# Decode attention, four layers: K tiles of two layers in halves, second query weights in two transfers, uneven first K pieces, mean from PSUM

## The chip, the cores and the metric

The kernel runs on one core of a Trainium2 chip. The metric is the device time of one launch in microseconds. A profile of one execution comes with the kernel; its engines are PE (TensorE matmuls), DVE (VectorE), ACT (ScalarE), POOL (GpSimd) and SP (SyncE, which here only issues DMAs and waits for their conditions).

## The reference

Four attention layers decode one token: A, B, A, B. A and B have their own K and V caches and weights; layer 2 uses A's again and layer 3 B's. All is bf16, with D = 640, 32 heads, 8192 keys and a head width of 192.

```python
def _A_ref(x, k_cache, v_cache, wq, wo):        # _B_ref computes the same
    q = (x @ wq).reshape(B, Sq, Hq, Dh).transpose(0, 2, 1, 3)
    scores = jnp.einsum("bhqd,bhkd->bhqk", q, k) * (Dh ** -0.5)
    p = _softmax(scores, axis=-1)
    o = jnp.einsum("bhqk,bhkd->bhqd", p, v)
    return o.transpose(0, 2, 1, 3).reshape(B, Sq, Hq * Dh) @ wo
x = x + _A_ref(_layernorm(x), A_k_cache, A_v_cache, A_wq, A_wo)
x = x + _B_ref(_layernorm(x), B_k_cache, B_v_cache, B_wq, B_wo)
x = x + _A_ref(_layernorm(x), A_k_cache, A_v_cache, A_wq, A_wo)
x = x + _B_ref(_layernorm(x), B_k_cache, B_v_cache, B_wq, B_wo)
```

K and V of one layer are 201 MB, so nearly all of the work is to stream them through the core once.

## The kernel before

**Tiles and slots.** A layer goes over 16 pairs of heads. A pair's K is a tile of 128 partitions (64 for each head) with 128 keys of 192 numbers on each, 6144 KB, and so is its V. SBUF holds eight slots of 3072 KB, half a tile each. A tile loads as one DMA where its two slots are adjacent and the tile is listed as joint, and otherwise as two. Slots 5 to 7 hold A's query weights (two and a half slots) from layer 0 to layer 2, and the second half of slot 7 the first quarter of A's first K tile. So layers 0 and 1 have slots 0 to 4, and their tiles are given slots by the strings `RINGS`, one word for each load, in the order of the plan. The last two V tiles of layer 1 stay in slots 0 to 3 until layer 3 needs them; layer 2 lives with slots 4 to 7, and layer 3 has all eight.

**The order.** `plan` is the order of the loads, and SP issues them strictly in that order; before each it waits for the steps in `before[n]`, which free what the slot held. A joint tile waits for both its slots. `steps` is the order of the work, which each compute engine follows in its own queue.

**The work of a pair.** *m* (`products`, L672, for each half): DVE multiplies the K half in place by the broadcast query (L687, in two or four chunks), and PE sums it over the 192 columns into a PSUM bank by matmuls with the identity (L702 and the helper's L72); the half is then free. *s* (`softmax`): DVE reduces the sums to scores (L742), takes the maximum, and ACT exponentiates (L757). *v* (`values`): PE multiplies the probabilities by V (L799 and L72); both halves are then free. *e* (`gather`): DVE picks and sums the diagonal blocks (L823, L825), and the row goes into `rows`. After every fifth pair, *wc* (`columns`) turns five pairs' outputs into columns and *wo* multiplies them by 2400 KB of output weights; the last pair's part is *wol* (480 KB). In layer 1 the last of the three is split: the first ten rows (*wo*), then five (*wob*).

**Between layers.** After *wol*, DVE adds the result to x (L907), sums x and its squares (L495, L496), PE adds over the partitions by a matmul with ones (L498), DVE scales by 1/640 (L501) and subtracts the mean (xb, L511). PE then computes q of the first pair (*lead*, L552), and the q of all other pairs in five rows c = 0 to 4 of the weights (*wq*, three groups of two, two and one rows, L575). Layer 1's query weights are one transfer of 7680 KB into slots 2, 3 and 4 (L440).

**Layer 2's first K tile** comes in quarters. The first is in SBUF already; the second and third go into slot 4, which holds layer 1's last output weights (ten rows, then *wob*, then *wol*, in this order), and the fourth into slot 5, over the first row of A's query weights (L421). The second waits for the ten rows' use, the third for *wol*'s, the fourth for the first group (two rows) of *wq*.

`busy` puts filler matmuls on PE (L487).

Of the kernel before, what the change touches and what calls it, by code (L numbers as in the profile page):

```python
# [69 lines left out]
def matmul_held(t, out, lhsT, rhs, start, stop, size=128, column=0):  # L70
# [10 lines left out]
RINGS = ["01 23 40 12 34 01 23 04 12 34 0 12 34 01 23 40 12 34 01 23 04 1 23 04 12 34 01 23 40 12 34 01 23 4 0 1",  # L81
         "234 01 23 40 12 34 01 23 04 12 34 0 12 34 01 23 40 12 34 01 23 04 1 23 04 12 34 01 23 40 12 34 01 23 4 01"]


def build(nc, A_x, A_k, A_v, A_wq, A_wo, B_x, B_k, B_v, B_wq, B_wo, out):
    _, H, SK, DH = A_k.shape
    D = A_x.shape[-1]
    P = 128
# [26 lines left out]
    with ExitStack() as ctx:  # L115
# [15 lines left out]
        QUARTER = [K0Q, slot[A_WQ - 1][:, 0:TS // 2], slot[A_WQ - 1][:, TS // 2:], slot[A_WQ][:, 0:TS // 2]]  # L131
        rows = sb("rows", [P, QR], BF16)
# [7 lines left out]
        small = sb("small", [P, 82], F32)  # L140
# [9 lines left out]
        neghalf = col(1)  # L150
        s_sb = [sb(f"s_sb{i}", [P, J], F32) for i in range(2)]
# [62 lines left out]
        PO.op(lambda g: g.memset(half33, 0.0))  # L214
        ev_const = PO.op(lambda g: g.memset(neghalf[:], -0.5))
# [35 lines left out]
        for l in range(NL):  # L251
            if l < 2:
                plan.append(("wq", l, 0))
                steps += [("wq", l, g) for g in range(3)]
            elif l == 2:
                steps += [("lead", l, 0, 0), ("wq", l, 0), ("lead", l, 0, 1), ("wq", l, 1), ("wq", l, 2)]
            else:
                both(("wq", l, 0))
            for p in range(NPAIR):
                if l == 0 and p == 0:  # L260
                    plan.append(("kh", l, p))
                if l == 2 and p == 0:
                    plan += [("kq", l, p, i) for i in range(1, 4)]
                else:
                    plan += [("k", l, p, u) for u in range(2)]
                if l == 2 and p == 0:
                    steps.append(("mq", l, p, 0))
                    for i in range(1, 4):
                        steps += [("mq", l, p, i), ("rd", l, p, i - 1)]
                    steps.append(("rd", l, p, 3))  # L270
                else:
                    steps.append(("m", l, p, 0))
                    if l == 2 and p == 1:
                        steps.append(("e", l, 0))
                    steps.append(("m", l, p, 1))
                if p == NPAIR - 1:
                    steps.append(("v", l, p - 1))
                steps.append(("s", l, p))
                if l == 3 and p == 0:
                    both(("wq", l, 1), ("wq", l, 2))  # L280
                if p < NPAIR - 2:
                    if first_load("v", l, p) == (l, p):
                        plan += [("v", l, p, u) for u in range(2)]
                    steps.append(("v", l, p))
                    if l != 2 or p > 0:
                        steps.append(("e", l, p))
                    if p + 1 in (PAIRS_W, 2 * PAIRS_W):
                        b = (p + 1) // PAIRS_W - 1
                        steps.append(("wc", l, b))
                        both(("wo", l, b))  # L290
            for i in (p - 1, p):
                if first_load("v", l, i) == (l, i):
                    plan += [("v", l, i, u) for u in range(2)]
            plan.insert(-2, ("wo", l, 2))
            steps += [("busy", l, 16), ("e", l, p - 1)] if NB[l] else [("e", l, p - 1)]
            steps += [("v", l, p, 0), ("wc", l, 2)] if NB[l] else [("wc", l, 2), ("v", l, p, 0)]
            steps += [("wo", l, 2), ("v", l, p, 1)]
            if NB[l]:
                plan.append(("vq", l))
                steps.append(("e", l, p))  # L300
                both(("wob", l))
            else:
                steps.append(("e", l, p))
            both(("wol", l))
            if l == 3:
                both(("woe", l))
        at = {n: i for i, n in enumerate(steps)}

        def released(n):
# [6 lines left out]
            return at[("wol", n[1]) if n[0] == "wo" and n[2] == 2 and NB[n[1]] else n]  # L316

        place, before, holder = {}, {}, [None] * NSLOT
        for g in range(3):
            place["wq", 0, g], before["wq", 0, g] = A_WQ + g, []  # L320
            holder[A_WQ + g] = ("wq", 2, g)
# [9 lines left out]
        def allot(n):  # L331
# [20 lines left out]
        for n in plan:  # L352
            if n[0] == "wol":
                before[n] = [] if NB[n[1]] else [("wc", n[1], 2)]
            elif n[0] in ("wob", "vq", "woe", "kh"):
                before[n] = []
            elif n[0] == "kq":
                before[n] = [None, ("woa", 1, 2), ("wo", 1, 2), ("wq", 2, 0)][n[3]:n[3] + 1]
                if n[3] == 3:
# [4 lines left out]
                    before["k", 2, 1, 1] = [("kq", 2, 0, 3)]  # L364
# [26 lines left out]
        def last_rows(l):  # L391

            return slot[place[("wo", l, 2)]][:, NW * D:(NW + OI) * D] if NB[l] else rows[:]
# [4 lines left out]
        def transfer(n):  # L398
# [10 lines left out]
            if n[0] == "wob":  # L409
                r0 = o["wo"][2] * PD  # L410
                return SP.op(lambda s: s.dma_start(
                    slot[place[("wo", l, 2)]][:, (NW - NB[l]) * D:NW * D],
# [4 lines left out]
            if n[0] in ("kh", "kq"):  # L417
                h = 2 * pair(l, 0)
                q = n[3] if n[0] == "kq" else 0
                r = w["k"][0, h:h + 2].rearrange("h (p j) d -> (h p) (j d)", j=J)[:, q * TS // 2:(q + 1) * TS // 2]  # L420
                return SP.op(lambda s: s.dma_start(QUARTER[q], r), *free, sem=[semVQ, *semR, semS[A_WQ]][q], inc=16)  # L421
            i = place[n]
            t = slot[i]
            if n[0] in "kv":
# [7 lines left out]
                if whole(*n[:3]):  # L432
                    if n[3] == 1:
                        return landed[n[:3] + (0,)]
                    x = TS // 2 if n[:3] == ("k", 0, 0) else 0
                    f = lambda s: s.dma_start(pool[:, i * TS + x:(i + 2) * TS], r[:, x:])
                else:
                    f = lambda s: s.dma_start(t, r[:, n[3] * TS:(n[3] + 1) * TS])
            elif n[0] == "wq" and l < 2:
                f = lambda s: s.dma_start(pool[:, i * TS:i * TS + DC * QW], w["wq"].rearrange("(p c) n -> p (c n)", c=DC))  # L440
# [51 lines left out]
        def sums(ev_z):  # L492

            DV.wait(ev_z, last["st"])
            DV.op(lambda v: v.tensor_reduce(st[:, 0:1], z[:], AX.X, ALU.add))  # L495
            e = DV.op(lambda v: v.scalar_tensor_tensor(out=zz[:], in0=z[:], scalar=1.0, in1=z[:],  # L496
                                                       op0=ALU.mult, op1=ALU.mult, accum_out=st[:, 1:2]))
# [3 lines left out]
            e = DV.op(lambda v: v.tensor_scalar(mv[:], TB[:, C_ST:C_ST + 2], 1.0 / D, None, ALU.mult), e, last["rs"], bank=TBu)  # L501
            last["stt"] = e
            return e

        def layer(l, ev_z, ev_true):

            ev_mv = sums(ev_z)
            if l == 0:
                ev_z = DV.op(lambda v: v.tensor_scalar(z[:], z[:], mv[:, 0:1], None, ALU.subtract), ev_mv)
                ev_mv = sums(ev_z)  # L510
            ev_xb = DV.op(lambda v: v.tensor_scalar(xb[:], z[:], mv[:, 0:1], None, ALU.subtract),  # L511
                          ev_mv, ev_z, last["xb"])
            if l == 2:
                busy(2)
            e = DV.op(lambda v: v.scalar_tensor_tensor(out=nv[:], in0=mv[:, 0:1], scalar=mv[:, 0:1], in1=mv[:, 1:2],
                                                       op0=ALU.mult, op1=ALU.subtract))
# [6 lines left out]
            if l < 3:  # L523
                ev_all = need(("wq", l % 2, 0))
                every = pool[:, place[("wq", l % 2, 0)] * TS:][:, 0:DC * QW].rearrange("p (c n) -> p c n", c=DC)
            if l == 1:
                q0 = (ORDER[3]["q0"] + 1 - LEAD[3]) * PD
                for c0, k in Q_PARTS:
                    ev_first[c0] = DV.op(lambda v, c0=c0, k=k: v.tensor_copy(
                        wq0[:, c0:c0 + k, :], every[:, c0:c0 + k, q0:q0 + LEAD[3] * PD]), ev_all)  # L530
# [13 lines left out]
            def q_lead(p, c0=0, c1=DC):  # L544

                if l < 3:
                    x, w, ev = pair(l, p) * PD, every, ev_all
# [10 lines left out]
            if l != 2:  # L558
                q_lead(0)

            def q_rows(g):

                n = ("wq", l, g)
                c0, k = Q_PARTS[g]
                t3 = wq_rows(l, g)[:, :, ORDER[l]["q1"] * PD if l < 3 else 0:]
                PE.wait(ev_all if l < 3 else need(n), ev_xb, last["O"], last["YB"], ev_first[c0] if l == 1 else None)
                for c in range(k):
                    todo = [(b, r, w) for b in range(4) for r in range(3)
                            for w in [min(512, QR - b * 512, QC[l] - r * QR - b * 512)] if w > 0]
                    for i, (b, r, w) in enumerate(todo):  # L570
# [6 lines left out]
                            signal=c == k - 1 and i == len(todo) - 1, bank=OYu)  # L577
                freed[n] = e
                if c0 + k == DC:
# [126 lines left out]
            def quarter(p, i):  # L706
# [5 lines left out]
                DV.wait(need(("kq", l, p, i) if i else ("kh", 0, 0)), ev_q[p])  # L712
# [138 lines left out]
            for n in [n for n in steps if n[1] == l]:  # L851
# [14 lines left out]
                elif n[0] == "lead":  # L866
                    q_lead(n[2], *((0, Q_PARTS[0][1]), (Q_PARTS[0][1], DC))[n[3]])
# [15 lines left out]
                elif n[0] == "wob":  # L883
                    last["oT"] = (project_row if l == 3 else project)(
                        n, slot[place[("wo", l, 2)]][:, (NW - NB[l]) * D:NW * D], oT[:, NW - NB[l]:NW], last["oTw"])
# [21 lines left out]
            ev_z = DV.op(lambda v: v.tensor_tensor(z[:], xc[:], YB[:, 0:DC], ALU.add), ev_y, ev_xc, bank=YBu)  # L907
# [62 lines left out]
```

## Time and profile before

| | |
|---|---|
| median of 3 runs | 1992.9 us (1992.61 to 1995.93) |
| the profiled execution | 1993.56 us, of which the span of the profile is 1991.8 us |
| PE busy | 1286.6 us (65%) |
| DVE busy | 1197.4 us (60%) |
| ACT busy | 168.6 us (8%) |
| read from HBM | 845.22 MB, 424 GB/s over the span |
| mean granted clock of PE | 0.789 |

How to read the views that follow. The page cuts the span into 40 slices of 49.8 us and gives the busy share of each in tenths. A row of the table by stretches has start and end, length, busy time of PE, its weight loads, DVE, ACT and POOL (instructions in brackets), granted clock, DMA share and GB/s. The DMA share is the time in which the 16 DMA engines had a packet in hand: a packet that takes long counts as busy, so that a stall within it shows in GB/s alone. A row of the timeline has start, duration, engine, line, operation, what it writes and reads, and in brackets the idle time before it with what ended it; "SPq" is SP issuing a DMA. A row of the chain has start, duration, and what the end of the program hung on at that time; a DMA there is the time from issue to landing. A row of the waits has the waiter, what it waited for, total, count, and longest.

### The profile page before, as it was taken

The page shows a single profiled execution, that of the slowest core. Times are in us where ns is not written, and L with a number is a line of the kernel's source. Part 1 is how long each engine was busy: PE and PEld are TensorE (multiplying, and loading weights), DVE is VectorE, ACT ScalarE, POOL GpSimd, SP SyncE. Part 2 cuts the span into 40 slices and gives each one's busy share as a digit, 9 for nine tenths or more (in the row PEclk, how much of TensorE's full clock was granted, in tenths as well). Part 3 has the DMA queues.
Part 4 walks back from the last instruction along what each step waited for, and adds up shares of the span by engine and source line. Part 5 has one row for each costly group of instructions (what it writes and reads, how often), then busy time and mean ns, then how long its engine had stood idle before and what let it go on. Part 6 is the DMA issues. An engine that isn't in the chain of part 4 may idle for free.

```text
span 1991.8 us, 12020 instructions
## 1 busy us (share of the span) xinstructions
PE 1286.6 (65%) x7741; PEld 129.5 (7%) x2601; DVE 1197.4 (60%) x817; ACT 168.6 (8%) x529; POOL 4.6 (0%) x24
## 2 busy tenths in 40 slices
PE   3475665666464665756686666666767667657568
PEld 0000000000200000010010000000002001000001
DVE  3565664677166565656656655756773666765656
ACT  0000000000100000000010000000000100000000
POOL 0000000000000000000000000000000000000000
PEclk9777877778687777778778877878787887778779
DMA  9999999999999999999999999999999999999998
GB/s 411 436 415 422 419 428 423 427 430 427 405 429 421 426 423 432 419 425 426 425 381 433 433 428 432 435 428 427 440 423 427 435 436 433 428 439 429 430 438 365
DMA packets 27959, 845.98 MB, mean 425 GB/s; under 512 B 3202, under 2 KB 3332, under 8 KB 3972
## 3 DMA queue, kind: packets, MB, share of 16 engines
q1 hardware_dynamic: 27764, 845.23, 99.2%
q8 instruction: 40, 0.66, 0.1%
q14 instruction: 11, 0.09, 0.0%
q10 hardware_dynamic: 144, 0.00, 0.0%
HBM read 845.22 MB, written 0.00 MB: 424 GB/s over the span
## 4 chain that ended last, share of the span: by engine, by line
DMA 54%; PE 25%; DVE 19%; ACT 1%; issue 0%; SPq 0%; DVEq 0%
DMA pool<-in_B_k_cache_dram 22%; PE S L72 16%; DMA pool<-in_A_k_cache_dram 15%; DVE pool L687 14%; DMA pool<-in_A_v_cache_dram 14%; PE OY L72 4%; DMA pool<-in_B_v_cache_dram 3%; PE OY L799 2%; DVE OY L823 1%; DVE acc L825 1%; DVE s_sb L742 1%; PE S L702 1%; ACT p_sb L757 1%; PE OY L637 1%; DVE pool L716 1%
## 5 line engine op out<-in xcount | busy, mean ns | idle before, releaser
L687 DVE TENSOR_TENSOR pool<-pool,q_sb 128x3072 bf16<-128x3072 bf16 (+2 forms) x364 | 837.6, 2368 | 167.9 <-DMA pool<-in_B_k_cache_dram 87.2
L72 PE MATMUL S<-pool,ident 128*128 128x512 bf16 x3006 | 790.4, 426 | 18.9 <-DVE pool L687 16.0
L823 DVE TENSOR_TENSOR OY<-OY,small 128x1536 f32<-128x1536 f32 x60 | 106.0, 1767 | 254.1 <-PE OY L72 254.0
L72 PE MATMUL OY<-pool,p_sb 128*16 128x512 bf16 x1920 | 208.4, 523 | 0.0
L837 PE MATMUL TB<-acc,small 128*33 128x192 f32 x120 | 44.4, 466 | 211.8 <-DVE acc L825 211.8
L702 PE MATMUL S<-pool,ident 128*128 128x512 bf16 x64 | 37.4, 584 | 218.5 <-DVE pool L687 218.5
L742 DVE TENSOR_REDUCE s_sb<-S 128x128 f32<-128x1024 f32 x63 | 77.2, 1225 | 157.4 <-PE S L72 157.4
L799 PE MATMUL OY<-pool,p_sb 128*16 128x512 bf16 (+1 forms) x1216 | 146.8, 506 | 36.1 <-DMA pool<-in_A_v_cache_dram 33.4
L541 ACT ACTIVATE q_sb<-QM 64x192 bf16<-64x192 f32 x118 | 38.4, 325 | 961.5 <-PE QM L589 960.8
L825 DVE TENSOR_REDUCE acc<-OY 128x192 f32<-128x1536 f32 x60 | 105.5, 1758 | 2.0
L846 ACT ACTIVATE rows<-TB,small 1x192 bf16<-1x192 f32 x120 | 49.5, 413 | 556.5 <-PE TB L837 555.0
L757 ACT ACTIVATE p_sb<-s_sb,small 64x128 bf16<-64x128 f32 x128 | 55.8, 436 | 167.0 <-DVE small L751 166.2
L747 PE MATMUL QM<-ident,m_bf 128*64 128x64 bf16 x128 | 14.0, 216 | 82.6 <-DVE m_bf L744 82.6
L813 DVE RECIPROCAL small<-TB 33x2 f32<-33x2 f32 x64 | 11.1, 173 | 92.4 <-PE TB L772 76.1
L772 PE MATMUL TB<-small,ones 128*33 128x2 f32 x120 | 14.5, 191 | 74.2 <-ACT p_sb L757 74.2
L589 PEld LDWEIGHTS QM<-rows,one_b 1*128 1x128 bf16 x59 | 5.4, 91 | 747.1 <-issue 747.1
L799 PEld LDWEIGHTS OY<-pool,p_sb 128*16 128x16 bf16 (+1 forms) x1216 | 35.7, 109 | 191.0 <-issue 146.7
L637 PE MATMUL OY<-pool,oT 128*1 128x320 bf16 x330 | 40.5, 427 | 2.2 <-ACT oT L667 2.2
L751 DVE TENSOR_REDUCE small<-QM 128x1 f32<-128x64 f32 x64 | 14.4, 225 | 30.2 <-PE QM L747 30.2
L837 PEld LDWEIGHTS TB<-acc,small 128*33 128x33 f32 x120 | 10.1, 130 | 300.2 <-DVE acc L825 300.2
L757 ACT ACTIVATION_READ_ACCUMULATOR p_sb<-s_sb,small 64x1 f32 x128 | 23.3, 182 | 0.0
L702 PEld LDWEIGHTS S<-pool,ident 128*128 128x128 bf16 x64 | 6.6, 103 | 253.0 <-DVE pool L687 252.4
(87 smaller groups left out, 253.4 us busy)
## 6 DMA issues: line engine op xcount, KB each, us to landing
pool<-in_B_k_cache_dram SPq DMA_DIRECT2D x27, 6144.0 KB, 31.8
pool<-in_B_v_cache_dram SPq DMA_DIRECT2D x25, 6144.0 KB, 26.2
pool<-in_A_v_cache_dram SPq DMA_DIRECT2D x24, 6144.0 KB, 23.8
pool<-in_A_k_cache_dram SPq DMA_DIRECT2D x36, 3072.0 KB, 19.9
pool<-in_A_k_cache_dram SPq DMA_DIRECT2D x12, 6144.0 KB, 19.0
pool<-in_A_v_cache_dram SPq DMA_DIRECT2D x16, 3072.0 KB, 17.3
pool<-in_B_k_cache_dram SPq DMA_DIRECT2D x10, 3072.0 KB, 20.1
pool<-in_B_v_cache_dram SPq DMA_DIRECT2D x8, 3072.0 KB, 20.4
```

The lines of the kernel that those rows point to most:

```text
L72: return t.add_instruction(mybir.InstMatmult(name=t.bass.get_next_instruction_name(), engine=mybir.EngineType.PE, ins=[t.lower_ap(rhs), t. ...
L541: lambda a, h=h, r=r, f=f: a.activation(q_sb[i][r, :], QM[r, h * DH:(h + 1) * DH], ACT.Copy, scale=f),
L637: e = PE.op(lambda t, i=i, h=h, f=l < 3 and n[2] == 0 and i == 0, fin=n == last_row and i == k - 1: t.matmul(YR[32 * h:32 * h + 1, :], lhs ...
L687: e = DV.op(lambda v, d0=d0, kin=kin, kout=kout, n=n: v.tensor_tensor(kout[:, :, d0:d0 + QD], kin[:, :, d0:d0 + QD], q_sb[qi][:, d0:d0 + Q ...
L702: t.matmul(S[:, :], lhsT=ident[:], rhs=k3[:, :, d0:d0 + R], start=d0 == 0, stop=fin)),
L742: lambda v: v.tensor_reduce(s[:], S_[:].rearrange("p (j r) -> p j r", r=R), AX.X, ALU.add),
L757: ev_p[p] = AC.op(lambda a, h=h, r=r: a.activation(p_sb[par][r, :, h], s[r, :], ACT.Exp, bias=negm[par][r, 0:1], accum_out=l_col[par][r, h ...
L799: t.matmul(o, lhsT=x, rhs=y, start=f, stop=fin) if c == 0 else
L823: e = DV.op(lambda v: v.tensor_tensor(o3, o3, pick[:, 0:VK].unsqueeze(2).broadcast_to([P, VK, DH]), ALU.mult), bank=Ou)
L825: e = DV.op(lambda v: v.tensor_reduce(acc[:], O.rearrange("p (i d) -> p d i", d=DH), AX.X, ALU.add), e, bank=Ou)
L837: e = PE.op(lambda t: t.matmul(TB[64:97, C_O:C_O + DH], lhsT=half33, rhs=acc[:], start=True, stop=True), bank=TBu)
L846: last["TO"] = last["row_written"] = AC.op(lambda a, h=h: a.activation(orow[:, o0 + h * DH:o0 + (h + 1) * DH], TB[64 + 32 * h:65 + 32 * h, ...
```

## The change

1. **K in halves.** In `RINGS` each K word of two slots becomes two words of one. The slots stay as they were, but each half of a K tile of layers 0 and 1 is now a transfer of its own that waits for its own slot. V stays joint where its slots are adjacent. The first K tile of layer 0 comes as a quarter, a quarter and a half.
2. **Second query weights.** Layer 1's transfer becomes two: rows 0 to 3 into slots 2 and 3 when these are free, row 4 into slot 4. The steps of *lead* and of the five rows are interleaved so that only the fifth chunk of *lead* and the rows after it wait for the second.
3. **Layer 2's first K.** The output weights of layer 1 move: *wob* to the end of slot 4, *wol* into `rows`, for which it waits for *wc*. The second piece of K grows from 6144 to 9024 numbers on each partition, on the same release; the third shrinks to 3264 and waits for *wob* instead of *wol*; the fourth waits for row 0 of *wq* alone. In layer 2, *lead* has its first chunk before row 0, the second before row 1, and three before row 2.
4. **Mean.** The addition to x also sums it (one instruction). The matmul is split into one for the sum and one for the squares, with 1/640 in its weights, and xb reads the mean from PSUM; a copy moves both to SBUF for the variance.

```diff
-RINGS = ["01 23 40 12 34 01 23 04 12 34 0 12 34 01 23 40 12 34 01 23 04 1 23 04 12 34 01 23 40 12 34 01 23 4 0 1",
-         "234 01 23 40 12 34 01 23 04 12 34 0 12 34 01 23 40 12 34 01 23 04 1 23 04 12 34 01 23 40 12 34 01 23 4 01"]
+RINGS = ["0 1 23 4 0 12 3 4 01 2 3 04 1 2 34 0 1 2 34 0 1 23 4 0 12 3 4 01 2 3 04 1 2 3 04 1 2 34 0 1 23 4 0 12 3 4 0 1 23 4 0 1",
+         "234 0 1 23 4 0 12 3 4 01 2 3 04 1 2 34 0 1 2 34 0 1 23 4 0 12 3 4 01 2 3 04 1 2 3 04 1 2 34 0 1 23 4 0 12 3 4 0 1 23 4 01"]
...
+        WOB = TS - NB[1] * D
+        AHEAD = WOB // DH * DH
+        PIECE = [(0, TS // 2, K0Q), (TS // 2, TS // 2 + AHEAD, slot[A_WQ - 1][:, 0:AHEAD]),
+                 (TS // 2 + AHEAD, 3 * TS // 2, slot[A_WQ - 1][:, AHEAD:]), (3 * TS // 2, 2 * TS, QUARTER[3])]
...
-            if l < 2:
-                plan.append(("wq", l, 0))
-                steps += [("wq", l, g) for g in range(3)]
-            elif l == 2:
-                steps += [("lead", l, 0, 0), ("wq", l, 0), ("lead", l, 0, 1), ("wq", l, 1), ("wq", l, 2)]
+            if l < 3:
+                plan += [("wq", l, 0), ("wq", l, 2)][:(1, 2, 0)[l]]
+                ahead_of = [{0: (0, DC)}, {0: (0, DC - 1), 2: (DC - 1, DC)}, {0: (0, 1), 1: (1, 2), 2: (2, DC)}][l]
+                for c in range(DC):
+                    steps += [("lead", l, 0, *ahead_of[c])] if c in ahead_of else []
+                    steps.append(("r", l, c))
...
-                if n[0] in "kv" and len(slots) == 2 and slots[1] == slots[0] + 1 and not halves:
+                if n[0] == "v" and len(slots) == 2 and slots[1] == slots[0] + 1 and not halves:
                     joint.add(n[:3])
-                put([n] if len(slots) == 1 else [n[:-1] + (u,) for u in range(len(slots))], slots, n[0] == "wq" or n[:3] in joint)
+                put([n] if len(slots) == 1 else [n[:-1] + (u,) for u in range(len(slots))], slots, n[:3] in joint)
+                if n == ("wq", 1, 0):
+                    before[n] = before[n] + before["wq", 1, 1]
...
-                before[n] = [] if NB[n[1]] else [("wc", n[1], 2)]
+                before[n] = [] if n[1] == 3 else [("wc", n[1], 2)]
...
-                before[n] = [None, ("woa", 1, 2), ("wo", 1, 2), ("wq", 2, 0)][n[3]:n[3] + 1]
+                before[n] = [None, ("woa", 1, 2), ("wob", 1), ("r", 2, 0)][n[3]:n[3] + 1]
...
             elif n[0] == "wq" and l < 2:
-                f = lambda s: s.dma_start(pool[:, i * TS:i * TS + DC * QW], w["wq"].rearrange("(p c) n -> p (c n)", c=DC))
+                a, b = (0, DC) if l == 0 else (0, DC - 1) if n[2] == 0 else (DC - 1, DC)
+                f = lambda s: s.dma_start(pool[:, i * TS:i * TS + (b - a) * QW],
+                                          w["wq"].rearrange("(p c) n -> p (c n)", c=DC)[:, a * QW:b * QW])
...
-        def sums(ev_z):
+        def sums(ev_z, summed):
...
-            e = PE.op(lambda t: t.matmul(TB[:, C_ST:C_ST + 2], lhsT=ones[:, 0:1].broadcast_to([P, P]), rhs=st[:], start=True, stop=True),
-                      e, ev_const, last["stt"], bank=TBu)
+            for i, e in enumerate((ev_st, ev_sq)):
+                e = PE.op(lambda t, i=i: t.matmul(TB[:, C_ST + i:C_ST + i + 1], lhsT=part_d.broadcast_to([P, P]),
+                                                  rhs=st[:, i:i + 1], start=True, stop=True), e, bank=TBu)
...
-            ev_xb = DV.op(lambda v: v.tensor_scalar(xb[:], z[:], mv[:, 0:1], None, ALU.subtract),
-                          ev_mv, ev_z, last["xb"])
+            ev_xb = DV.op(lambda v: v.tensor_scalar(xb[:], z[:], TB[:, C_ST:C_ST + 1], None, ALU.subtract),
+                          ev_mean, ev_z, last["xb"], bank=TBu)
...
-            ev_z = DV.op(lambda v: v.tensor_tensor(z[:], xc[:], YB[:, 0:DC], ALU.add), ev_y, ev_xc, bank=YBu)
+            ev_z = DV.op(lambda v: v.scalar_tensor_tensor(out=z[:], in0=xc[:], scalar=1.0, in1=YB[:, 0:DC], op0=ALU.mult, op1=ALU.add,
+                                                          accum_out=st[:, 0:1]), ev_y, ev_xc, last["st"], bank=YBu)
```

More of the change, by code (lines that the diff above doesn't have):

```diff
@@ L391, in last_rows, with block_rows @@
         def last_rows(l):
-            return slot[place[("wo", l, 2)]][:, NW * D:(NW + OI) * D] if NB[l] else rows[:]
+            return slot[place[("wo", l, 2)]][:, NW * D:(NW + OI) * D] if l == 3 else rows[:]
+        def block_rows(l):
+            t = slot[place[("wo", l, 2)]]
+            return t[:, WOB:] if l == 1 else t[:, (NW - NB[l]) * D:NW * D]
         def quarters(n):
@@ L546, in q_lead @@
                 if l < 3:
-                    x, w, ev = pair(l, p) * PD, every, ev_all
+                    x, w, ev = pair(l, p) * PD, every, ev_all[c0]
                 else:
@@ L883, in layer @@
                 elif n[0] == "wob":
[L884 to L885 removed]
+                    last["oT"] = freed[n] = (project_row if l == 3 else project)(
+                        n, block_rows(l), oT[:, NW - NB[l]:NW], last["oTw"])
                 elif n[0] == "woe":
```

76 lines of the change are left out of this document (47 added, 29 removed).

## The prediction

> **What bounds the kernel now.** I read the page first, then busy time and bandwidth by stage, then the chain that ended last.
>
> ```profile
> span 1991.8 us, 12020 instructions
> ...
> PE 1286.6 (65%) x7741; PEld 129.5 (7%) x2601; DVE 1197.4 (60%) x817; ACT 168.6 (8%) x529; POOL 4.6 (0%) x24
> ...
> DMA  9999999999999999999999999999999999999998
> ```
>
> The DMA engines are busy in every slice; no compute engine is busy over 65%. So the time is bytes over rate, plus the stretches in which the queue is short of work. The change moves no bytes, and only a better rate or less idle queue can pay. By layer (the last two columns are DMA share and GB/s):
>
> ```profile
> 1.76:514.30 512.54, 313.80 (x1853) 29.88 (x576) 299.19 (x197) 42.81 (x132) 2.02 (x11) 0.79 0.99 424
> 512.00:516.00 4.00, 3.47 (x44) 2.51 (x44) 0.00 (x0) 0.43 (x1) 0.00 (x0) 0.83 0.68 226
> 515.70:1028.00 512.30, 323.94 (x1972) 32.39 (x672) 298.84 (x191) 41.80 (x132) 0.55 (x1) 0.76 1.00 425
> 1028.00:1042.00 14.00, 13.35 (x130) 4.23 (x77) 5.01 (x14) 2.96 (x4) 0.55 (x1) 0.68 0.79 297
> 1042.20:1511.20 469.00, 310.45 (x1748) 26.25 (x525) 295.59 (x223) 38.41 (x127) 0.00 (x0) 0.80 1.00 431
> 1520.00:1942.00 422.00, 276.49 (x1649) 25.73 (x499) 266.56 (x167) 37.86 (x118) 0.55 (x1) 0.79 1.00 433
> ```
>
> Layers 0 and 1 run at 424 and 425 GB/s, layers 2 and 3 at 431 and 433, though layer 0 reads the same K and V as layer 2. Between the layers stand two dips, 226 and 297. The chain says why layers 0 and 1 are slow:
>
> ```profile
> 107.76 18.92 DMA pool<-in_A_k_cache_dram
> ...
> 126.70 3.37 DVE pool L687
> ...
> 130.73 7.52 PE S L72 x23
> ...
> 138.26 17.95 DMA pool<-in_A_k_cache_dram
> ...
> 156.24 13.18 DVE pool L687 x4
> ...
> SPq L436 <- PE S L72: 366.4, 21, 23.7
> ```
>
> A K tile of 6.29 MB is issued when the first half of the K tile before it has been consumed; it lands 18.9 us later, its first half is consumed 11.6 us after that, and the next K goes out: 30.5 us a turn (107.76 to 138.26). K and V of a pair, 12.58 MB, need 29.2 us at 431 GB/s. So the latency of a whole K tile sets the pace there, and the queue has just run dry when K arrives: the transfer issued at 138.26 takes 17.95 us where 6.29 MB at 431 are 14.6. The last row, of the DMA queue's own waits, counts 21 such issues.
>
> **The change, part by part.** First the sizes, from the list of issues:
>
> ```profile
> pool<-in_B_k_cache_dram SPq DMA_DIRECT2D x27, 6144.0 KB, 31.8
> pool<-in_A_k_cache_dram SPq DMA_DIRECT2D x36, 3072.0 KB, 19.9
> pool<-in_A_k_cache_dram SPq DMA_DIRECT2D x12, 6144.0 KB, 19.0
> pool<-in_B_wq_dram SPq DMA_DIRECT2D x1, 7680.0 KB, 21.1
> pool<-in_A_wo_dram SPq DMA_DIRECT2D x6, 2400.0 KB, 18.9
> ```
>
> *K in halves (layers 0, 1).* The slots stay the same; the 12 whole tiles of A, its shortened first one, and 13 of B's 27 (the other 14 are layer 3's) become two transfers each. With the query weights that is 27 issues more. Each half waits for its own slot alone. Worked for one pair p at 431 GB/s (a half is 7.3 us), K.0(p) landing at 0: K.1 lands at 7.3, V at 21.9, K.0(p+1) at 29.2. A half is consumed 11.5 us after it lands (126.70 to 138.26), V about 5.3 us after:
>
> ```profile
> 116.32 0.60 PE L799 MATMUL OY<-pool,p_sb 128*16 128x512 bf16 x4
> 121.66 1.77 DVE L823 TENSOR_TENSOR OY<-OY,small 128x1536 f32<-128x1536 f32 x1 [5.06 <-PE OY L72]
> 123.46 1.76 DVE L825 TENSOR_REDUCE acc<-OY 128x192 f32<-128x1536 f32 x1
> ```
>
> With five slots each half reuses the slot of five halves ago. K.0(p+1) waits for V(p-1), long gone. K.1(p+1) waits for K.0(p), free at 11.5, and its first byte is due at 29.2: 17.7 us in hand. V(p+1), still joint, waits for V(p), free at 27.2, due at 36.5: 9.3 in hand. Before, the joint K(p+1) waited for K.0(p), free at 11.5 after a landing of the whole tile, and was due at 14.6: 3 us on paper, less the landing delay. So the K loop goes, and what is late next is V by 9 us of margin, which is no loss. Layer 2 already runs this mix (K in 3072 KB halves, V joint) with four slots, at 431; that row is the rate I take, the overhead of more and smaller transfers included.
>
> A layer is 32 tiles of 6144 KB, 7680 KB of query and 7680 KB of output weights: 217.1 MB, at 431 GB/s 503.6 us. Layer 0 took 512.5: gain 8.9, of which I leave out 0.8, the share of the first 48 us, in which no K tile has yet waited for a K tile. Layer 1 took 512.3: gain 8.7. Ends: at 433, layer 3's whole-tile rate, 2.3 more in each layer; at the old 424.5, nothing.
>
> [...]
>
> *Second query weights in two transfers (layer 0 to 1).*
>
> ```profile
> 499.15 1.77 DVE L823 TENSOR_TENSOR OY<-OY,small 128x1536 f32<-128x1536 f32 x1
> 505.65 0.33 SPq L406 DMA_DIRECT2D rows<-in_A_wo_dram  x1
> 514.76 0.33 SPq L440 DMA_DIRECT2D pool<-in_B_wq_dram  x1
> 517.44 0.33 SPq L436 DMA_DIRECT2D pool<-in_B_k_cache_dram  x1
> ```
>
> Before, the 7680 KB wait for three slots, the last held by the output weights until 514.76, when the queue is already dry (226 GB/s in 512 to 516). After, the first 6144 KB need the two slots of V of pair 14, done by 499; SP stands in order behind the issue at 505.65, so they go out at about 506, and run 14.6 us. The last 1536 KB (514.76) and K (517.44) then queue behind them. Gain: the 1.4 us between 514.30 and 515.70, the rest of the dip being inside layer 0's 512.5. The added wait, for the last 1536 KB, holds on PE the fifth lead matmul and query rows 2 to 4; they come 3.7 us after the first piece, and rows 0 and 1 (3.4 us, below) fill that. Behind them wait q of pair 0 and the first V; K's first half lands 7 us later still, so it costs nothing; uncovered it would be under 1 us.
>
> *Uneven pieces, output weights moved (layer 1 to 2).*
>
> ```profile
> 1024.12 0.33 SPq L421 DMA_DIRECT2D pool<-in_A_k_cache_dram  x1
> 1029.22 1.16 PE L603 MATMUL OY<-oT,pool 128*128 128x1 bf16 x25
> 1031.01 0.33 SPq L421 DMA_DIRECT2D pool<-in_A_k_cache_dram  x1
> 1033.53 0.59 PE L575 MATMUL OY<-pool,xb 128*1 128x512 bf16 x3
> 1036.93 0.33 SPq L421 DMA_DIRECT2D pool<-in_A_k_cache_dram  x1
> 1039.24 0.33 SPq L438 DMA_DIRECT2D pool<-in_A_v_cache_dram  x1
> ```
>
> The three pieces (4.72 MB, 10.9 us at 431) stretch over 14.2 us, 1028 to 1042.2: 3.3 lost. After, the first is 2.31 MB (5.4 us) on the same release at 1024.12, so the queue lasts to about 1033.5; the second (1.9 us) goes out after the 25 matmuls ending at 1030.4, in time. The third waits for one row of query weights instead of two (3.4 us for both, 1033.53 to the old release at 1036.93), and one of two lead matmuls less stands before it: about 1034.9, due at 1035.5, thin. The V half after it still waits for row 3, 1039.2, and is due at 1039.1: about 1 us idle. Gain 1.7, bounds 0 and 3.3. The last 480 KB of output weights now wait for the columns step, which PE runs before the weights whose end releases the first piece at 1024.12; only that piece is queued behind: nothing.
>
> *Mean from PSUM.* One matmul and a copy more, a reduction and a scaling less, xb perhaps 0.4 us earlier (an estimate: of the seven steps in the 1.3 us from the weights' end at 1031.01 to xb at 1032.32 two go). Only the 1031 boundary could feel it, and there filler matmuls stand on PE before the lead:
>
> ```profile
> 1031.95 0.59 PE L487 MATMUL S<-ident 128*128 128x512 bf16 x1
> 1032.32 0.23 DVE L511 TENSOR_SCALAR xb<-small 128x5 bf16<-128x5 f32 x1
> 1032.75 0.85 PE L552 MATMUL QM<-pool,xb 128*128 128x384 bf16 x2
> ```
>
> Nothing, within 0.4 either way; elsewhere query weights or a full queue cover it.
>
> Sum: 8.1 + 8.7 + 1.4 + 1.7 = 19.9 us. The profiled execution took 1993.56 (span 1991.8 and 1.8 around it), so 1973.7; the median of the runs lies 0.7 lower, at 1992.9: **1973**. Layers 2 and 3 keep their transfers, and start 20 us earlier.
>
> **Rivals.** (a) *V takes K's place.* V stays joint and its 9.3 us can shrink where it is split or the output weights come between; if half the starved pairs stay so, 8.4 of the 16.8 us are lost: 1981.4. For it: thin margins are what the page shows; against it: layer 2, with a slot fewer, does not starve.
>
> (b) *The rate belongs to the layers, not to the wait.* Then only the boundaries pay, 3.1 us: 1990. Against it: layers 0 and 2 read the same tensors.
>
> (c) *Compute becomes the bound, slower.* A pair costs 28.8 us of compute in layer 0 (DVE from 96.40, the K tile's start, to 125.2), and 28.0 in layer 3 where nothing waits for DMA:
>
> ```profile
> 96.40 13.16 DVE L687 TENSOR_TENSOR pool<-pool,q_sb 128x6144 bf16<-128x6144 bf16 x4 [6.86 <-DMA pool<-in_A_k_cache_dram]
> 379.53 7.71 PE S L72 x23
> 1554.92 1.78 DVE OY L823
> 1695.13 1.78 DVE OY L823
> ```
>
> (140.21 over five pairs.) PE now gets K in two bursts. If that drops its clock so that both halves take the slowest 7.71 instead of 12.7 together, a pair costs 31.5; a pair's bytes at the old 424 GB/s take 29.7, which is the point from which it loses: 1.8 us by 32 pairs, 58 slower, about 2048. Against it: layer 2 consumes halves at a mean clock of 0.80.
>
> (d) *Every transfer pays its latency.* 17.95 less 14.6 is 3.4 us for a transfer on a dry queue; unhidden, 27 times that is 92 us: 2082. It decides only where the queue is dry. Against it: layer 2's 30 halves (36 less three pairs of layer 0) would cost 100 of its 469 us.
>
> **How the numbers follow.** My forecast 0.75, (a) 0.13, (b) 0.04, (c) 0.04, (d) 0.02; 0.02 for within noise. The forecast's own range goes from 1968 (433 GB/s) to 1978 (one term of 8 halved, and the boundary at nothing); to hold 8 in 10 with (a) the range is 1968 to 1983. About 0.2%, 4 us, is what a measurement can tell from no change. Faster 0.91, same 0.03, slower 0.06.
>
> **What would show it.** Right: both first layers at 429 to 433 GB/s; the queue's wait for PE at whole tiles nearly gone; no dip at the first boundary and about 350 in the 14 us of the second; the chain in layers 0 and 1 through V, not K. Wrong: GB/s there still under 427, issues of V or of K halves late in numbers, or, for (c), a longer S group and a chain of PE and DVE without DMA.

## The result, and the profile after

The changed kernel takes 1977.8 us (median of six runs, 1977.5 to 1979.58) where the kernel before takes 1994.63 beside it: a ratio of 0.9917, 95% interval 0.9904 to 0.993. The profiled execution took 1977.52 us against 1993.56, which is 16.0 less; the forecast was 19.9 less and 1973. The sign, the mechanism and the range held, and 3.9 us of the gain are missing (3.1 by the medians, which lie 16.8 apart).

From the page of the changed kernel:

```profile
span 1975.6 us, 12068 instructions
...
PE 1298.4 (66%) x7751; PEld 132.1 (7%) x2611; DVE 1197.8 (61%) x817; ACT 168.3 (9%) x529; POOL 4.6 (0%) x25
...
DMA  9999999999999999999999999999999999999998
```

The engines are about as busy as before, and DMA alone is full. By layer, in stretches that answer to those of the prediction (the last two columns are DMA share and GB/s):

```profile
1.76:510.00 508.24, 325.34 (x1883) 32.45 (x610) 299.36 (x197) 42.73 (x132) 2.06 (x12) 0.79 1.01 431
510.00:1015.00 505.00, 327.93 (x1978) 33.32 (x674) 299.14 (x191) 41.72 (x132) 0.55 (x1) 0.79 1.00 429
1015.00:1027.00 12.00, 11.61 (x121) 3.80 (x68) 4.65 (x13) 2.92 (x4) 0.55 (x1) 0.78 0.84 319
1027.00:1500.00 473.00, 310.33 (x1792) 28.65 (x571) 296.07 (x223) 38.80 (x129) 0.00 (x0) 0.80 1.00 431
1510.00:1925.00 415.00, 273.17 (x1616) 23.75 (x471) 264.61 (x156) 36.75 (x115) 0.00 (x0) 0.78 1.00 432
```

Layers 0 and 1 now run at 431 and 429, like layers 2 and 3; only the second boundary still dips. To see where the time came from, both kernels have to be cut at the same places. Before, then after:

```profile
2.00:485.00 483.00, 291.72 (x1662) 23.53 (x455) 284.44 (x185) 40.39 (x124) 1.82 (x11) 0.79 1.00 424
485.00:530.00 45.00, 27.21 (x255) 9.40 (x184) 16.82 (x25) 2.69 (x9) 0.55 (x1) 0.75 0.93 391
530.00:1000.00 470.00, 295.07 (x1675) 24.61 (x471) 281.79 (x165) 39.54 (x124) 0.00 (x0) 0.76 1.00 426
1000.00:1046.00 46.00, 42.06 (x390) 9.80 (x233) 24.00 (x31) 4.95 (x11) 0.55 (x1) 0.82 0.92 379
```

```profile
2.00:485.00 483.00, 310.44 (x1706) 25.44 (x461) 295.26 (x192) 40.31 (x124) 1.86 (x12) 0.79 1.00 429
485.00:530.00 45.00, 23.11 (x257) 9.96 (x201) 7.50 (x20) 3.24 (x11) 0.55 (x1) 0.70 1.00 426
530.00:1000.00 470.00, 309.97 (x1745) 24.70 (x478) 293.00 (x173) 39.89 (x127) 0.00 (x0) 0.79 1.00 431
1000.00:1046.00 46.00, 34.97 (x367) 10.29 (x236) 20.35 (x28) 5.59 (x13) 0.55 (x1) 0.89 0.96 395
```

A stretch of length L at G GB/s has lost L x (1 - G/431) against a full queue. The differences are 5.6 us in layer 0 (424 to 429), 3.7 at the first boundary (391 to 426), 5.5 in layer 1 (426 to 431) and 1.7 at the second boundary (379 to 395): 16.5 together. A long row is uncertain by about 1 us: cut at 4 and 486 instead, layer 0 has 426 and 430, which is 4.5 us. Each stretch begins where the other kernel has moved other bytes, so this is bookkeeping by rate, not tile by tile.

The chain in layers 0 and 1 now goes through V in place of K; one K half stands in it in each layer (issued at 316.32 and 938.90). Some of its rows, from layer 0 and then from layer 1:

```profile
86.15 24.67 DMA pool<-in_A_v_cache_dram
...
143.36 25.81 DMA pool<-in_A_v_cache_dram
```

```profile
713.72 24.34 DMA pool<-in_B_v_cache_dram
...
743.44 23.76 DMA pool<-in_B_v_cache_dram
...
771.73 24.61 DMA pool<-in_B_v_cache_dram
```

Two pairs take 57.2 us in layer 0 (86.15 to 143.36) and 58.0 in layer 1 (713.72 to 771.73), 28.6 and 29.0 for one, where the bytes need 29.2 at 431 GB/s and a turn before was 30.5. The wait of whole tiles for PE's sums, which stood at 366.4 us in 21 issues, is nearly gone, as forecast (the first row below). Single halves and joint V tiles wait for PE instead; at 429 to 431 GB/s these waits cost next to nothing:

```profile
SPq L453 <- PE S L72: 37.3, 3, 12.9
...
SPq L456 <- PE S L72: 548.5, 45, 34.3
SPq L453 <- PE OY L72: 519.5, 45, 19.7
```

L456 issues a single half, L453 a joint tile.

### The profile page after: what moved, and what is told of

It reads as the page before. It is cut to its first block, busy times and chain, and to the rows that moved or that the text cites. A ratio compares the mean times of both kernels' runs of the same rounds, so it can differ in the third digit from the quotient of the medians.

```text
span 1975.6 us, 12068 instructions
## 1 busy us (share of the span) xinstructions
PE 1298.4 (66%) x7751; PEld 132.1 (7%) x2611; DVE 1197.8 (61%) x817; ACT 168.3 (9%) x529; POOL 4.6 (0%) x25
## 4 chain that ended last, share of the span: by engine, by line
DMA 65%; PE 18%; DVE 15%; ACT 1%; issue 0%; SPq 0%
DMA pool<-in_A_v_cache_dram 29%; DMA pool<-in_B_v_cache_dram 17%; DMA pool<-in_B_k_cache_dram 13%; DVE pool L719 11%; PE OY L72 7%; PE S L72 6%; DMA pool<-in_A_k_cache_dram 5%; PE OY L831 4%; DVE OY L855 1%; DVE acc L857 1%; DMA pool<-in_B_wq_dram 1%; DVE s_sb L774 1%; DVE pool L748 1%; ACT p_sb L789 1%; PE S L734 0%
## 5 line engine op out<-in xcount | busy, mean ns | idle before, releaser
L72 PE MATMUL OY<-pool,p_sb 128*16 128x512 bf16 x1920 | 220.1, 550 | 0.0
L831 PE MATMUL OY<-pool,p_sb 128*16 128x512 bf16 (+1 forms) x1216 | 152.5, 524 | 78.6 <-DMA pool<-in_A_v_cache_dram 53.1
L804 PE MATMUL TB<-small,ones 128*33 128x2 f32 x120 | 14.6, 192 | 74.1 <-ACT p_sb L789 74.1
```

The costliest lines, as they stand in the source:

```text
L72: return t.add_instruction(mybir.InstMatmult(name=t.bass.get_next_instruction_name(), engine=mybir.EngineType.PE, ins=[t.lower_ap(rhs), t. ...
L831: t.matmul(o, lhsT=x, rhs=y, start=f, stop=fin) if c == 0 else
```

## The experiments

Twelve kernels, of which one repeats the changed kernel. Its median there was 1979.48 (1977.71 to 1980.23), so one program's median moves by 1.7 us between sets of runs, and a difference to the changed kernel below 2 us is not read as one unless both were run in the same set. Two letters in the first expectations need a word. S is the theory that layers 0 and 1 gained all that was forecast and lost it again at the second boundary; the spread of the DMA engines, from which it takes its name, is the author's guess, and no trace or run shows it. C is that the waits which the change adds at that boundary lose the time. (In the last experiment C is another theory, named there.)

**Parts alone and undone.** Halves alone, on the kernel before:

```diff
-RINGS = ["01 23 40 12 34 ...
+RINGS = ["0 1 23 4 0 12 3 4 ...
...
-                if n[0] in "kv" and len(slots) == 2 and slots[1] == slots[0] + 1 and not halves:
+                if n[0] == "v" and len(slots) == 2 and slots[1] == slots[0] + 1 and not halves:
```

> The kernel before with K halves in layers 0 and 1 alone; query weights in one transfer, old pieces, old mean. Theory S (spread): halves keep the queue full in both layers and are worth about 19 us there, but an unbroken queue lets the 16 DMA engines drift apart, so that the last V of layer 1 lands some 5 us behind the bytes' mean and the second boundary loses more than before; the first boundary also runs dry, since the joint query weights wait for the output weights: about 1983 us, 11 less than before. The prediction's terms (16.8 for the halves, nothing lost elsewhere): 1977.5. If halves were not what pays: 1991 or more.

Measured 1981.37 (1980.27 to 1982.03) against 1992.81 before, ratio 0.9936 (0.9923 to 0.9948): 11.4 us, not the 16.8 that the prediction's two terms add up to. Its stretches say where they went:

```profile
2.00:485.00 483.00, 303.71 (x1702) 24.08 (x457) 295.37 (x192) 40.36 (x124) 1.83 (x11) 0.81 1.00 429
485.00:530.00 45.00, 17.64 (x214) 9.24 (x182) 6.20 (x18) 2.69 (x9) 0.55 (x1) 0.65 0.91 385
530.00:985.00 455.00, 299.58 (x1688) 25.01 (x471) 284.85 (x167) 39.51 (x124) 0.00 (x0) 0.78 1.00 431
```

The layers run at the changed kernel's rates, which is 5.6 and 5.5 us by the rows above, and the boundaries lose little or nothing by it: the first has 385 GB/s for 391, the second (1000 to 1046) 390 for 379. So the missing part was not gained in the layers and lost again at the second boundary, as S has it; the layers never held it.

The changed kernel with the two lines above turned back, K whole in both layers:

> The changed kernel with K of layers 0 and 1 whole again; the query weights in two transfers, uneven pieces and new mean stay. All theories that put the gain into the halves: 1990 to 1992, the 3.1 us that the prediction gave the two boundaries, and 424 to 425 GB/s in layers 0 and 1. If the boundaries were the larger part: under 1986.

Measured 1988.73 (1987.38 to 1992.39), ratio 0.9976 (0.9964 to 0.9987). The other three parts alone are worth 4.1 us beside 1992.81; the forecast had 3.1. Layers 0 and 1 are at 424 and 426 GB/s again.

The changed kernel with the second query weights in one transfer:

```diff
-                plan += [("wq", l, 0), ("wq", l, 2)][:(1, 2, 0)[l]]
+                plan += [("wq", l, 0)][:(1, 1, 0)[l]]
...
```

> The changed kernel with the second query weights in one transfer that waits for all three slots. The prediction's term: 1.4 us slower, 1979. Theory S: after halves the compute is no longer ahead of the queue by as much as the queue is by compute, the queue is dry from about 506 to the release at 509 and one first byte later, 3.5 to 4 us slower, of which up to 1 comes back at the second boundary because the stop brings the engines together: 1980.5 to 1982.

Measured 1981.72 (1980.6 to 1982.01), ratio 0.9937 (0.9923 to 0.995): 2.2 to 3.9 slower than the changed kernel. Its issue of the query weights, those of the changed kernel (two, the second at 509.18), and its first boundary:

```profile
509.89 0.33 SPq L459 DMA_DIRECT2D pool<-in_B_wq_dram  x1
```

```profile
499.06 10.45 SPq L459 DMA_DIRECT2D pool<-in_B_wq_dram  x2
```

```profile
485.00:530.00 45.00, 17.97 (x216) 9.49 (x184) 6.57 (x19) 2.69 (x9) 0.55 (x1) 0.66 0.91 381
```

381 for 426 is 4.7 us. The whole dip comes back, so the two transfers are worth about 4 us there (2.2 to 3.9 by the times, 3.7 and 4.7 by the rows), and halves do not hide it.

The changed kernel with layer 2's first K in equal quarters, with the old waits and places of the output weights:

```diff
-        WOB = TS - NB[1] * D
-        AHEAD = WOB // DH * DH
+        WOB = (NW - NB[1]) * D
+        AHEAD = TS // 2
...
-                before[n] = [None, ("woa", 1, 2), ("wob", 1), ("r", 2, 0)][n[3]:n[3] + 1]
+                before[n] = [None, ("woa", 1, 2), ("wol", 1), ("wq", 2, 0)][n[3]:n[3] + 1]
...
```

> The changed kernel with layer 2's first K in equal quarters again, on the old releases, and the output weights of layer 1 in their old place without the wait for the columns step. The prediction's term: 1.7 us slower. Theory S: the second boundary is now bound by the chain from the last V's landing to row 3 of the query weights, which frees the slot of layer 2's first V; the pieces move that by little: 0.5 to 1 slower. Rival C (the changed waits themselves lost the time at the second boundary): 1 to 4 us faster than the changed kernel, 1974 to 1977.

Measured 1979.61 (1978.62 to 1980.52), ratio 0.9927 (0.9914 to 0.9939): 1.8 slower than the changed kernel's first median and 0.1 than its second. C has fallen: without the new waits nothing is won back. Since pieces and waits were undone together, neither is priced alone, and what the two gain is not told apart from nothing by the time.

The changed kernel with sum and mean as before:

> The changed kernel with the old mean (sums in one reduction and one matmul, scaled on DVE). The prediction: nothing, within 0.4 us. By the two traces xb started 1.31 us after the last weights before and 1.52 after at the second boundary, where PE runs four passes for the two sums behind the filler: 0 to 0.3 us faster than the changed kernel.

Measured 1977.78 (1976.88 to 1978.83), ratio 0.9914 (0.99 to 0.9928): no difference to the first median, as forecast. The profile of the changed kernel shows xb no earlier after the weights' end:

```profile
1016.86 0.16 DVE L942 SCALAR_TENSOR_TENSOR small<-small,OY 128x5 f32<-128x5 f32 x1 [2.83 <-PE OY L635]
...
1018.38 0.24 DVE L539 TENSOR_SCALAR xb<-small,TB 128x5 bf16<-128x5 f32 x1 [1.14 <-PE TB L520]
```

1.52 us from the addition to xb, where the kernel before needed 1.31 (1031.01 to 1032.32): xb still waits for PE, on which the fillers stand.

To price each layer by itself, K whole in layer 1 alone, K whole in layer 0 alone, and the changed kernel again, in one set of runs:

```diff
-                if n[0] == "v" and len(slots) == 2 and slots[1] == slots[0] + 1 and not halves:
+                if n[0] in ("v", "vk"[n[1]]) and len(slots) == 2 and slots[1] == slots[0] + 1 and not halves:
...
```

(For layer 0 it is "kv". The old `RINGS` line of the layer concerned comes with it.)

> The changed kernel with layer 1's K tiles whole again (layer 0's stay in halves). Theory L (the bandwidth by stretches, 426 before and 431 after over the 470 us from 530 to 1000, is worth 5.5 us; the forecast's 8.7 for layer 1 was too large because it set the stretch's length against the layer's bytes alone): 5.5 us slower than the changed kernel, less about 1 us that the second boundary gives back, so 4 to 6 slower, about 1982 to 1984; GB/s in 530 to 1000 back at 426 to 427. The prediction's term: 8.7 slower, 1986.5. Theory B (the miss lies at the second boundary, where halves cost 3 us or more): only 2 to 3 slower or less, because the boundary would gain what the layer loses.

> The changed kernel with layer 0's K tiles whole again (layer 1's stay in halves). Theory L: the stretch from 2 to 485 us falls from 429 to 424 GB/s, which is 5.6 us; the first boundary stays full by its two transfers, so 5 to 6.5 us slower than the changed kernel, about 1983 to 1984. The prediction's term: 8.1 slower, 1986. Halves in the two layers together cost 11 us when undone; L expects the two runs to add up to 10 to 12.

> The changed kernel unaltered, on the same chip as the two runs above, so that they are compared with it directly: 1977 to 1979.5 by every theory; 431 GB/s from 530 to 1000 and about 395 from 1000 to 1046.

Measured 1983.98 (1979.95 to 1987.04) for layer 1, 1982.92 (1980.32 to 1984.56) for layer 0 and 1979.48 for the repeat: 4.5 and 3.4 us. The stretches of the layer concerned, first with layer 1 whole, then with layer 0 whole, then the repeat:

```profile
530.00:1000.00 470.00, 294.69 (x1680) 23.45 (x457) 289.09 (x167) 39.29 (x124) 0.00 (x0) 0.77 1.00 424
1000.00:1046.00 46.00, 40.13 (x385) 10.48 (x237) 22.98 (x31) 5.59 (x13) 0.55 (x1) 0.85 0.95 385
```

```profile
2.00:485.00 483.00, 293.54 (x1665) 24.67 (x459) 285.50 (x186) 40.31 (x124) 1.86 (x12) 0.79 1.00 426
```

```profile
2.00:485.00 483.00, 307.10 (x1706) 25.29 (x461) 295.51 (x192) 40.31 (x124) 1.86 (x12) 0.80 1.00 430
530.00:1000.00 470.00, 312.47 (x1740) 24.93 (x475) 293.37 (x173) 39.61 (x126) 0.00 (x0) 0.78 1.00 431
1000.00:1046.00 46.00, 35.62 (x342) 10.24 (x232) 20.14 (x28) 5.59 (x13) 0.55 (x1) 0.83 0.94 381
```

The layer that is whole falls back to about the rate it had before (424 for 426 in layer 1, 426 for 424 in layer 0) and the other keeps its own: the rate follows how K is loaded, layer by layer. Layer 1's 4.5 is within the 4 to 6 of theory L; layer 0's 3.4 is below its 5 to 6.5 (whole K ran at 426 here, not at 424), and the two add up to 7.9 where L expected 10 to 12. Both are about half of the prediction's 8.7 and 8.1. The prices are rough: the runs with layer 1 whole spread over 7 us, and the profiled one, at 1985.64, is 6.2 slower than the repeat's, with 7.6 lost in its row (424 for 431). Theory B's give-back of 3 us or more at the second boundary is not there: 385 beside the repeat's 381 is 0.4 us. A give-back of 1 or 2 us is not excluded, since the kernel with both layers whole had 403 there, beside the changed kernel's 395 and 381.

**The second boundary.** Does an unbroken queue lose there? The changed kernel with a stop late in layer 1, for which the first half of its last K also waits for the K before:

```diff
+                if n == ("k", 1, 15, 0):
+                    before[n] = before[n] + [("k", 1, 14, 0)]
```

> The changed kernel with one stop of the DMA queue late in layer 1: the first K half of pair 15 also waits until pair 14's first K half is consumed (965.9 instead of 944.7, first byte due at 960.2 to 965.5), so most DMA engines stand still for 4 to 6 us there. Theory S (spread): the late engines set the landing of the last V, the stop costs the early ones alone, and the second boundary gives back what the stop takes: only 1 to 2.5 us slower than the changed kernel, and the last V quarter lands within 2 us of the bytes' mean. Rival C (the loss at the second boundary is in the chain and its waits, whatever the engines do): the stop comes on top, 4 to 6.6 us slower.

Measured 1985.48 (1983.79 to 1987.39), ratio 0.9954 (0.994 to 0.9967): 7.7 slower than the changed kernel's first median (and than the kernel with the old mean, in the same set) and 6.0 than its second, far above what S allows.

```profile
955.00:972.00 17.00, 13.37 (x50) 0.29 (x3) 15.79 (x10) 0.82 (x2) 0.00 (x0) 0.80 0.58 236
```

```profile
1000.00:1046.00 46.00, 39.56 (x370) 10.37 (x231) 21.34 (x28) 5.59 (x13) 0.55 (x1) 0.81 0.96 399
```

The stop itself costs 7.7 us (236 GB/s over 17 us), and the boundary gets back 0.4 of it (399 for 395), or 1.9 beside the repeat's 381. S has fallen: most of a stop ahead of the boundary is lost.

Is it the release of V's first half that counts? The changed kernel with the query rows in the order 2, 3, 0, 1, 4, which frees V's slot first, and V issued ahead of the fourth K piece; and the same without the four filler matmuls at this boundary:

```diff
+                    steps += [("lead", 2, 0, 2, 4), ("r", 2, 2), ("r", 2, 3), ("lead", 2, 0, 0, 2), ("lead", 2, 0, 4, 5),
+                              ("r", 2, 0), ("r", 2, 1), ("r", 2, 4)]
...
+        plan[i:j + 1] = [plan[j]] + plan[i:j]
...
```

> The changed kernel with layer 2's query rows in the order 2, 3, 0, 1, 4 (lead's chunks 2 and 3 before them), and its first V half issued ahead of the fourth K piece: what the second boundary waits for last is then free one lead and two rows sooner. If the chain from the last V to the first V half of layer 2 is the bound there (theory S): about 3 us faster, 1974 to 1975.5. If the bytes or the spread alone bound the boundary: 0 to 1 faster.

> e6 without the four filler matmuls around the mean of layer 2. The fillers hold the mean's matmul 0.4 us and the first lead matmul 0.4 us behind data that are ready, so 0.8 us faster than e6 if PE's granted clock stays; if the clock falls to 0.5 without them the rows take up to twice 0.8 us each and it is 1 to 3 us slower than e6.

Measured 1979.27 (1978.97 to 1979.55) and 1979.22 (1979.15 to 1979.32), ratio 0.9921 for both: 1.5 slower than the kernel with the old mean in the same set and level with the repeat, not faster. V goes out earlier, 1022.72 for 1024.36, but now nothing fills the time until then, since the fourth piece stands behind it; the changed kernel issues that piece at 1020.88:

```profile
1022.72 0.33 SPq L463 DMA_DIRECT2D pool<-in_A_v_cache_dram  x1
1024.21 0.33 SPq L446 DMA_DIRECT2D pool<-in_A_k_cache_dram  x1
```

The stretch from 1000 to 1046 is at 378 GB/s. We read this as: what counts is when the queue gets its next bytes of any kind; no run shows that by itself. The fillers make no difference to the time.

The repeat shows another thing. The same program loses 5.3 us in 1000 to 1046 (381 GB/s) where it lost 3.8 (395), and the granted clock of PE differs, 0.83 and 0.89. Around the boundary, in the changed kernel's first profile and in the repeat:

```profile
1010.00:1018.00 8.00, 5.37 (x74) 3.88 (x74) 1.21 (x7) 0.27 (x1) 0.00 (x0) 0.50 0.97 369
1018.00:1022.00 4.00, 4.00 (x31) 0.71 (x13) 0.81 (x5) 0.00 (x0) 0.55 (x1) 0.71 0.73 253
```

```profile
1018.00:1022.00 4.00, 4.00 (x24) 0.61 (x10) 0.81 (x5) 0.00 (x0) 0.55 (x1) 0.50 0.56 227
1022.00:1026.00 4.00, 4.00 (x48) 0.50 (x12) 1.15 (x1) 0.83 (x2) 0.00 (x0) 0.83 0.97 344
```

The second of the query rows on PE and the issue of V, from the two timelines in the same order:

```profile
1021.26 0.76 PE L72 MATMUL OY<-pool,xb 128*1 128x512 bf16 x9
...
1024.36 0.33 SPq L456 DMA_DIRECT2D pool<-in_A_v_cache_dram  x1
```

```profile
1021.92 1.38 PE L72 MATMUL OY<-pool,xb 128*1 128x512 bf16 x9
...
1025.69 0.33 SPq L456 DMA_DIRECT2D pool<-in_A_v_cache_dram  x1
```

PE is at half its clock from its wait for the last V on: in both profiles that wait (1.71 and 1.65 us) ends near 1011.6, and the clock is 0.50 from 1010 to 1018. In the first profile it is 0.50 from 1018 to 1020.3 and 1.00 from 1020.3 to 1022. If it steps as sharply in the repeat, 0.83 in 1022 to 1026 puts the step there near 1023.4, an estimate. The nine matmuls take 1.38 us instead of 0.76, and V goes out 1.3 us later. So the last kernel puts fillers ahead of it, to see whether they hold the clock up:

```diff
-                        if l == 3:
+                        if l in (1, 3):
                             busy(6)
...
-                if end and l == 3:
+                if end and l in (1, 3):
                     busy(3)
...
+                    if n == ("v", 1, NPAIR - 1, 0):
+                        busy(3)
```

> The changed kernel with twelve more filler matmuls on PE at the end of layer 1: three ahead of the last pair's sums (L808), six ahead of the last V quarter, three while DVE gathers. Theory C (at the second boundary the releases of the K pieces and of V wait for PE at half its clock: in the changed kernel's profile the clock is 0.51 from 1010 and rises near 1020, in the repeated one only near 1023.5, and V's first half is issued at 1024.36 and 1025.69): with the clock held up, the rows take 0.8 us each instead of up to 1.7, the fourth K piece is issued 0.5 to 2 us earlier and V's first half by 1022.5 to 1023.5; GB/s in 1000 to 1046 from 395 and 381 to 400 or more; the time 1 to 3 us less than the changed kernel's 1977.8 and 1979.48, so 1975.5 to 1977.5. Rival D (the clock falls while PE waits for V whatever stands there, or the fillers put off the chain by as much as they gain): issues within 0.5 us of the repeated run's and 1977.5 to 1980.

Measured 1979.02 (1977.14 to 1980.6), ratio 0.9931 (0.9918 to 0.9945): no faster.

```profile
1010.00:1018.00 8.00, 7.49 (x93) 3.71 (x80) 2.02 (x12) 0.27 (x1) 0.10 (x1) 0.97 0.99 372
1018.00:1022.00 4.00, 4.00 (x31) 0.49 (x10) 0.00 (x0) 0.04 (x1) 0.44 (x1) 0.63 0.89 318
1000.00:1046.00 46.00, 38.73 (x380) 9.92 (x239) 20.55 (x29) 5.60 (x13) 0.55 (x1) 0.93 0.98 395
```

```profile
1018.03 1.38 PE L72 MATMUL OY<-pool,xb 128*1 128x512 bf16 x9
...
1023.67 0.33 SPq L456 DMA_DIRECT2D pool<-in_A_v_cache_dram  x1
```

The clock was 0.97 until 1018, then fell all the same, and the first query row's nine matmuls took 1.38 us again. V was issued at 1023.67, 0.7 and 2.0 us earlier than in the two profiles without these fillers, but the stretch is at 395, no more than the better of them. So the fillers did not keep the clock up where the rows run, V was earlier all the same, and no gain shows; neither C nor D came out whole. What sets the 4 to 5 us that remain at this boundary is not settled. No version was clearly faster than the changed kernel.

## Why the prediction was right or wrong, point by point

**The K loop** was what bound layers 0 and 1, as said: alone, undone, and undone by layers, halves move the time by 11.4, 9 to 11, and 3.4 and 4.5 us, and the rate with them. Two things change with a half: it waits for one slot alone, and its consumption starts before the rest of its tile has landed. No run has one without the other. A smaller transfer is not faster as such: layer 3's whole tiles run at 432 GB/s. The rate taken from layer 2 (431) is what both layers reached, and V is in the chain without a loss. Of its 9.3 us of margin an estimated 6 to 8 are left: the V rows shown above take 23.76 to 25.81 us from issue to landing, of which the bytes need 14.6 and a transfer on a dry queue 3.4 more (17.95 less 14.6).

**The step that failed is the size of the two K terms, 8.1 and 8.7.** Layer 0's was taken over a stretch to 514.30 that held most of the first boundary's dip. With the 1.4 counted for that boundary it was 9.5; the rows give 5.6 and 3.7, together 9.3, so this error was only one of where, and the query weights were worth about 4 us rather than 1.4. Layer 1's is really too large. The stretch's length, 512.3, was set against the layer's bytes at 431, 503.6; but its own row says 425 GB/s, and 512.3 x (1 - 425/431) is 7.1. The stretch held some bytes that the count of the layer left out. Then the changed layer was supposed to run at 431 to its end, while 510 to 1015 ran at 429, another 2.3 at that row's rounding. 7.1 less 2.3 is 4.8; the rows give 5.5 over the steady part, the undone layer 4.5 by its median and 6.2 by its profiled execution. So the term was 2.5 to 4.2 us too large, 3.2 by the rows, and with that it is most of the 3.9 that are missing.

**The uneven pieces** were given 1.7 within 0 to 3.3. The two profiles give 1.7 (379 to 395), but the repeat 0.2 (381), and the undone pieces 0.1 to 1.8 by the time (377 GB/s in the same stretch). The term stays inside its bounds and is not measured better than that. The trace of before had PE at half clock in this place too (0.50 from 1026 to 1034); a release that is computed from one such profile carries this uncertainty with it. About 350 GB/s was expected there; 319 is what the 12 us from 1015 show.

**The mean** was put at nothing, and no difference shows.

**The rivals.** (a) V takes K's place in the chain, without its loss. (b) is refuted by the layers one by one. (c) PE is busy 11.8 us longer over the span and binds nothing. (d) 27 transfers more and the kernel is faster, at 429 to 431 GB/s in the layers that have them, so the 3.4 us that a transfer on a dry queue took besides its bytes (17.95 less 14.6) are hidden there: 27 times that, the 92 us of (d), are nowhere in this trace.

## What to carry to other kernels

A transfer should wait for no more than the buffer it overwrites: a tile that waits for two buffers and lands whole before its first half is used closes a loop through its own latency (here 30.5 us a turn, for bytes that need 29.2 at 431 GB/s), and the page shows this only as a rate of 424 where another layer has 431. Size such a gain by the rate of the stretch itself, cut both at places away from the boundaries, and count the boundaries apart; a length set against a list of bytes collects the neighbours' idle time and bytes. And repeat the profile before explaining a difference of 1 or 2 us at one place.

## What was not expected of the hardware

One program, profiled twice, had PE's clock come back to full about 3 us apart at the second boundary (at 1020.3, and by the estimate above near 1023.4), and its DMA rate there was 395 and 381 GB/s. The two profiles show that the point of the rise varies between executions, and not why. With the fillers, PE was busy for 7.49 of the 8 us before 1018, at a clock of 0.97, and the clock still fell to 0.63 over the next 4 us, all of them busy; why it fell there stays open.
